# An instruction scheduler inside a kernel: forward and backward passes, durations nearer to the trace, and a new place for the late weight loads

## The chip, the cores and the metric

One core of a Trainium2 chip runs the whole program in one launch. The metric is the device time of one execution in microseconds. A first group of three runs of the kernel before gave a median of 398.55 us (397.55 to 398.92). Executions are compared within one state. All runs told here had a mean granted TensorE clock of 0.994 to 1.0 and are in the fast state; a program that was run only once has no state, and that is said where it comes. A mean of 0.996 is not the same as one of 1.0, though: in the kernel before such runs are slower by 1.7 us, as the part on calls 2 and 3 shows.

Five engines work in parallel: TensorE (PE in the profile) multiplies matrices into PSUM; ScalarE (ACT) and VectorE (DVE) read PSUM and work on SBUF; GpSimd (POOL) works on SBUF; SyncE (SP) only issues DMA transfers here. Each has its own list of instructions and waits on semaphores for the others. The order of those five lists is what this change is about.

## The reference

Two attention layers and two feed-forward (GLU) layers alternate, each with a layer norm before it and a residual addition after it. The sequence is 2048 rows of 512 columns, all in bfloat16.

```python
def _A_ref(x, wqkv, w_phi, wo):            # H = 32 heads of 16
    q, k, v = ...                          # x @ wqkv, split in heads
    pq = einsum("bhsd,hdf->bhsf", q, w_phi); pk = einsum(... k, w_phi)
    phi_q = concat([softmax(pq), softmax(-pq)]); phi_k = the same of pk
    kv  = einsum("bhsf,bhsd->bhfd", phi_k, v)      # needs every key row
    num = einsum("bhqf,bhfd->bhqd", phi_q, kv)
    den = einsum("bhqf,bhf->bhq", phi_q, sum of phi_k over s) + 1e-6
    return (num / den) ... @ wo
def _B_ref(x, W_gate, W_up, W_down):       # 512 -> 1376 -> 512
    gate = x @ W_gate; gate = gate * (gate > 0)
    return (gate * (x @ W_up)) @ W_down
# ...
x = x + _A_ref(_layernorm(x), ...);  x = x + _B_ref(_layernorm(x), ...)
x = x + _A_ref(_layernorm(x), ...);  x = x + _B_ref(_layernorm(x), ...)
```

One fact of it shapes everything below: `kv` sums over all 2048 rows, so no row can get its `num` before the last key tile has been through its softmax. The first attention layer therefore has a key stage, then a narrow place, and only then the long streams of GLU matmuls.

## The kernel before

The program is written as a list of operations. Each names its engine, what it reads and writes, and a duration in nanoseconds that the author gives it. A scheduler then simulates the five engines with these durations and so decides the order of each engine's list. Nothing else of the simulation reaches the chip; only the order does. The scheduler of before goes through the program once, with one ranking:

```python
class Program:
    ORDER_WEIGHT = 20.0
    DMA_BW = 300.0
    # ...
    def schedule(self):
        # ...
        rank = [0.0] * n                  # the longest way from here to the end
        for o in reversed(ops):
            rank[o.idx] = o.dur + max([rank[q] + lat(o, ops[q]) for q in succ[o.idx]], default=0.0)
        prio = [self.ORDER_WEIGHT * o.idx - rank[o.idx] - o.boost for o in ops]
        # ... one forward pass: of what can start soonest, take the lowest prio
```

The parts whose durations the change touches, and the loads whose place it touches:

```python
    # normalising the keys: the whole tile on POOL, for the last two tiles half on DVE
    parts = [("pool", 0, 2)] if t < NT - 2 else [("pool", 0, 1), ("dve", 1, 2)]
    # ... expk = expk * rZk
       (1930 if s1 - s0 == 2 else 980) if eng == "pool" else 620, f"{tag} phik {t} {s0}")
# ...
    # layer norm's "apply" on DVE: ytile = x * rstd - mean * rstd
       [r("x", t), r("mv", t), r("rstd", t)], [r("yt", yb)], 407, f"{tag} apply {t}")
# ...
        def kv(t, n):                     # emit(): key tiles t .. t+n-1
            # ... projections
            for tt in range(t, t + n):
                self.kv_acc(tt, "A0")
                for _ in range(2):        # two late weight loads per key tile
                    if pieces:
                        pieces.pop(0)(self.r("phik", tt, 0))
        # ...
        kv(10, 2)
        self.q_proj(0, qr0, "A0")         # queries of the first 512 rows
        kv(12, 2)
        kv(14, 1)
        kv(15, 1)
        self.kv_fin("A0")                 # kvbd: kv out of PSUM, masked
        for li in (0, 2):
            # ...
            N([0, 1, 2, 3])               # num, divide, wo, residual, layer norm
            for st in range(1, NSLAB):
                self.q_proj(st, qring, A, [self.r("expk", 15, 1)], w=2)
            # ... then GLU steps mixed with the rest of the num steps
```

The late weights (`pieces`) are the twenty-two loads of wo, Wg, Wu and Wd that are not needed at the start. Each is held back until a given key tile has been normalised.

The softmax here doesn't subtract the row's maximum and nothing guards it: scores larger than these inputs give would overflow.

## Time and profile before

| | before |
|---|---|
| median of 3 runs | 398.55 us |
| the profiled run, and its span in the trace | 397.03 us, 395.1 us |
| TensorE busy | 380.4 us (96%), 2320 matmuls |
| VectorE, ScalarE, GpSimd busy | 274.2, 217.5, 111.2 us |
| DMA | 23 MB, 58 GB/s over the span |

Most of the reading of this profile is in the prediction below. Two views are added here, because the result turns on them. In a timeline the columns are start in us, length in us, engine, line and operation, the tiles, how many in a row, and in brackets the engine's idle time before it and what ended it. The first is the timeline of ACT just after the keys of the first layer. L590 is the exponential of the queries, and L607 is the copy of `num` out of PSUM, three copies to a tile.

```profile
55.06 1.02 ACT L590 ACTIVATE expq<-ps 128x1024 bf16<-128x1024 f32 x1 [3.37 <-PE ps L587]
55.98 1.32 ACT L607 ACTIVATE numbf<-ps 128x432 bf16<-128x432 f32 x3
57.20 1.02 ACT L590 ACTIVATE expq<-ps 128x1024 bf16<-128x1024 f32 x1
58.10 0.96 ACT L607 ACTIVATE numbf<-ps 128x432 bf16<-128x432 f32 x2
59.26 0.41 ACT L607 ACTIVATE numbf<-ps 128x288 bf16<-128x288 f32 x1 [0.19 <-PE ps L603]
```

ACT stands idle for 3.37 us, then does one exponential, the three copies of tile 0, another exponential, and the three copies of tile 1. The second is the timeline of TensorE near the end, the down projections of the last GLU:

```profile
383.67 2.98 PE L678 MATMUL ps<-Wd,hT 128*128 128x512 bf16 x13
386.99 4.93 PE L678 MATMUL ps<-Wd,hT 128*128 128x512 bf16 x22 [0.34 <-DVE x_sb L680]
```

TensorE waits there for a residual addition to clear a PSUM bank.

### The profile page before, as it was taken

To read this page: it belongs to the slowest core of one execution; us is meant where nothing else is said; L and a number is where in the kernel's file an instruction comes from. 1 tells how busy PE (TensorE), PEld (TensorE's weight loads), DVE (VectorE), ACT (ScalarE), POOL (GpSimd) and SP (SyncE) were. 2 spreads that over 40 slices of the span, in tenths; PEclk is the share of its full clock that TensorE was granted. 3 is DMA by queue.
4 is the path that set the end of the run, shared out by engine and by line. 5 is a ranking of instruction groups with operands and counts; after the bars stand their busy time and mean duration, and the time that the engine had idled before them with its cause. 6 is when DMAs were issued, how large, how long until landed. Compare 5 with 4: busy or idle time off the path is not lost.

```text
span 395.1 us, 6306 instructions
## 1 busy us (share of the span) xinstructions
PE 380.4 (96%) x2320; PEld 206.0 (52%) x2320; DVE 274.2 (69%) x634; ACT 217.5 (55%) x421; POOL 111.2 (28%) x160
## 2 busy tenths in 40 slices
PE   5999987999999999999999999899999999999996
PEld 3445543676744544444444467467774454444442
DVE  4999868778767898887747876977776677222222
ACT  5989759753735513532454483996474562452440
POOL 5389931112000213373334552120301101000000
PEclk9999999999999999999999999999999999999999
DMA  6845841322211222301000110231322132100001
GB/s 208 207 87 126 258 135 27 68 53 55 42 40 27 42 41 57 73 18 28 13 13 2 27 28 2 44 73 32 75 56 60 40 42 66 42 13 26 2 27 53
DMA packets 61518, 23.00 MB, mean 58 GB/s; under 512 B 53456, under 2 KB 60464, under 8 KB 61488
## 3 DMA queue, kind: packets, MB, share of 16 engines
q1 hardware_dynamic: 60912, 22.08, 24.1%
q10 hardware_dynamic: 576, 0.52, 0.5%
q8 instruction: 18, 0.29, 0.3%
q14 instruction: 12, 0.10, 0.1%
HBM read 7.91 MB, written 2.10 MB: 25 GB/s over the span
## 4 chain that ended last, share of the span: by engine, by line
PE 86%; DMA 4%; DVE 3%; ACT 3%; issue 2%; POOL 1%; ACTq 0%; SPq 0%; DVEq 0%
PE ps L654 39%; PE ps L678 19%; PE ps L633 7%; PE ps L514 7%; PE ps L587 5%; PE ps L603 3%; PE ps L545 3%; PE ps L560 2%; DMA x_sb<-in_A_x_dram 2%; ACT expk L548 1%; DMA yT<-ytile 1%; DMA hT<-in_A_wqkv_dram 1%; ACT expq L590 1%; DVE expk L531 1%; ACT numbf L607 1%
## 5 line engine op out<-in xcount | busy, mean ns | idle before, releaser
L654 PE MATMUL ps<-yT,Wg 128*128 128x512 bf16 (+3 forms) x440 | 127.6, 336 | 0.0
L654 PE MATMUL ps<-yT,Wu 128*128 128x512 bf16 (+3 forms) x440 | 124.0, 336 | 0.0
L678 PE MATMUL ps<-Wd,hT 128*128 128x512 bf16 (+1 forms) x352 | 107.9, 379 | 0.3 <-DVE x_sb L680 0.3
L656 ACT ACTIVATE gate_sb<-ps 128x512 bf16<-128x512 f32 (+3 forms) x110 | 56.4, 514 | 93.8 <-PE ps L654 85.5
L478 POOL TENSOR_SCALAR rv<-mv 128x1 f32<-128x1 f32 (+1 forms) x55 | 14.1, 258 | 192.2 <-DVE mv L475 192.2
L531 POOL TENSOR_TENSOR expk<-expk,rZk 128x1024 bf16<-128x1024 bf16 (+1 forms) x32 | 59.6, 1879 | 27.0 <-DVE rZk L528 21.1
L654 PEld LDWEIGHTS ps<-yT,Wu 128*128 128x128 bf16 (+1 forms) x440 | 43.9, 100 | 33.2 <-ACT expk L661 0.9
L654 PEld LDWEIGHTS ps<-yT,Wg 128*128 128x128 bf16 (+1 forms) x440 | 43.5, 100 | 33.5 <-ACT gate_sb L656 0.6
L607 ACT ACTIVATE numbf<-ps 128x432 bf16<-128x432 f32 (+1 forms) x96 | 44.9, 496 | 19.9 <-PE ps L603 19.1
L678 PEld LDWEIGHTS ps<-Wd,hT 128*128 128x128 bf16 (+1 forms) x352 | 34.2, 98 | 37.1 <-DVE x_sb L680 1.0
L663 DVE TENSOR_TENSOR hT<-gate_sb,expk 128x512 bf16<-128x512 bf16 (+3 forms) x73 | 25.8, 354 | 32.5 <-ACT expk L661 32.4
L474 DVE BATCH_NORM_STATS2 stats<-x_sb 128x6 f32<-128x512 bf16 x64 | 42.6, 680 | 5.5 <-DMA x_sb<-in_A_x_dram 5.2
L526 DVE TENSOR_REDUCE Zk<-expk 128x64 f32<-128x1024 bf16 x32 | 38.1, 1205 | 6.6 <-ACT expk L517 5.2
L633 PE MATMUL ps<-wo_p,oT 128*128 128x512 bf16 x128 | 38.8, 379 | 0.5 <-DMA oT<-osb 0.5
L603 PE MATMUL ps<-kvbd,expq 128*128 128x144 bf16 x256 | 35.8, 226 | 2.0 <-ACT numbf L607 1.5
L590 ACT ACTIVATE expq<-ps 128x1024 bf16<-128x1024 f32 (+1 forms) x40 | 32.7, 863 | 8.5 <-PE ps L587 8.4
L587 PE MATMUL ps<-yT,Wqp 128*128 128x512 bf16 x128 | 35.8, 379 | 1.7 <-ACT expq L590 1.7
L661 ACT ACTIVATE expk<-ps 128x512 bf16<-128x512 f32 (+3 forms) x73 | 36.3, 498 | 1.6 <-PE ps L654 1.0
L680 DVE TENSOR_TENSOR x_sb<-x_sb,ps 128x512 bf16<-128x512 bf16 x32 | 21.6, 683 | 21.5 <-PE ps L678 21.2
L479 POOL TENSOR_TENSOR rstd<-rv,mhalf 128x1 f32<-128x1 f32 (+1 forms) x55 | 34.1, 621 | 4.1
L666 DVE TENSOR_TENSOR hT<-gate_sb,ps 128x512 bf16<-128x512 bf16 (+2 forms) x37 | 22.6, 611 | 16.3 <-PE ps L654 12.2
L517 ACT ACTIVATE expk<-ps 128x512 bf16<-128x512 f32 x44 | 23.7, 602 | 18.2 <-PE ps L514 18.0
(57 smaller groups left out, 400.1 us busy)
## 6 DMA issues: line engine op xcount, KB each, us to landing
out_dram<-x_sb SPq DMA_DIRECT2D x16, 128.0 KB, 1.7
x_sb<-in_A_x_dram SPq DMA_DIRECT2D x3, 512.0 KB, 6.6
Wg<-in_B_W_gate_dram SPq DMA_DIRECT2D x4, 344.0 KB, 3.6
Wu<-in_B_W_up_dram SPq DMA_DIRECT2D x4, 344.0 KB, 6.0
Wd<-in_B_W_down_dram SPq DMA_DIRECT2D x5, 256.0 KB, 7.0
yT<-ytile SPq DMA_TRANSPOSE x60, 2.4
hT<-in_A_wqkv_dram ACTq DMA_DIRECT2D x4, 128.0 KB, 3.0
x_sb<-in_A_x_dram SPq DMA_DIRECT2D x4, 128.0 KB, 3.7
```

What stands on the lines that cost most here:

```text
L474: op("dve", (lambda t: lambda e: e.bn_stats(k.stats6[:, t, :], k.x_sb[:, t, :]))(t), [r("x", t)], [r("st", t)], 685, f"{tag} stats {t}")
L526: op("dve", lambda e: e.tensor_reduce(k.Zk[:, zb, :], k.expk[:, t, :, :].rearrange("p s (h f) -> p (s h) f", f=16), AX.X, ALU.add), [r("ex ...
L531: op(eng, (lambda s0, s1: lambda e: e.tensor_tensor(k.expk[:, t, s0:s1, :].rearrange("p s (h f) -> p (s h) f", f=16), k.expk[:, t, s0:s1, ...
L587: op("pe", (lambda c, ic, bank: lambda e: e.matmul(k.pb[bank][:], k.Wqp[:, ic, c * 128:(c + 1) * 128], k.yT[:, ic, st * 512:(st + 1) * 512 ...
L590: op("act", (lambda c0, s, b0: lambda e: e.activation(k.expq[:, st, c0:c0 + w, s, :], k.ps[:, b0:b0 + w, :], ACT.Exp, scale=(1.0 - 2.0 * s ...
L603: op("pe", (lambda s, c, j, g0, bank: lambda e: e.matmul(k.pb[bank][:, j * GW:(j + 1) * GW], k.expq[:, st, c, s, tt * 128:(tt + 1) * 128], ...
L607: op("act", (lambda g0, n, bank: lambda e: e.activation(k.numbf[:, b, g0:g0 + n, :], k.pb[bank][:, 0:n * GW].rearrange("p (g m) -> p g m", ...
L633: op("pe", (lambda c, bank: lambda e: e.matmul(k.pb[bank][:], k.oT[:, ob, c, :], k.wo_p[:, c, :], start=(c == 0), stop=(c == NC - 1)))(c, ...
L654: op("pe", (lambda bank, W, ic, fc, Mf: lambda e: e.matmul(k.pb[bank][0:Mf, 0:n], W[:, ic, fc * 128:fc * 128 + Mf], k.yT[:, ic, c0:c0 + n] ...
L656: op("act", (lambda Mf, gb, gs: lambda e: e.activation(k.gate_sb[0:Mf, gs, 0:n], k.pb[gb][0:Mf, 0:n], ACT.Relu))(Mf, gb, gs), [self.RP[gb] ...
L661: op("act", (lambda Mf, ub, tu: lambda e: e.activation(k.expk[0:Mf, tu, 0, 0:n], k.pb[ub][0:Mf, 0:n], ACT.Copy))(Mf, ub, tu), [self.RP[ub] ...
L678: op("pe", (lambda fc, Kf, u, c0: lambda e: e.matmul(k.pb[bank][:], k.hT[0:Kf, u, c0:c0 + 128], k.Wd[0:Kf, fc, :], start=(fc == 0), stop=( ...
```

## The change

The change has three parts, and none adds, removes or resizes an operation.

1. **A search in place of one pass.** Four weights of the ranking start it. For each, a forward pass makes a schedule; a backward pass then schedules the same program from its end and gives each operation a time at which it would come if everything were as late as it can be; these times are the ranking of the next forward pass. There are twelve passes for each weight, 48 in all, and the schedule with the shortest simulated time is kept.
2. **Durations set nearer to those of the trace.** A few operations and loads get other durations in the model, among them the key multiply on DVE (1050 instead of 620 ns; in the trace of before it takes from 0.69 to 2.03 us) and the DMA bandwidth (240 instead of 300 bytes per ns).
3. **Late weights over more key tiles.** Tiles 4 to 11 release one late load each instead of two.

```diff
-    ORDER_WEIGHT = 20.0
-    DMA_BW = 300.0
+    ORDER_WEIGHTS = (5.0, 10.0, 20.0, 30.0)
+    PASSES = 12
+    DMA_BW = 240.0
@@ schedule
-        prio = [self.ORDER_WEIGHT * o.idx - rank[o.idx] - o.boost for o in ops]
+        best = None
+        for weight in self.ORDER_WEIGHTS:
+            prio = [weight * o.idx - rank[o.idx] - o.boost for o in ops]
+            for _ in range(self.PASSES):
+                start, finish, order = self._forward(prio)
+                span = max(finish)
+                if best is None or span < best[0]:
+                    best = (span, start, finish, order)
+                prio = [t - o.boost for t, o in zip(self._backward(start, finish), ops)]
 (... _forward is the old pass, made a function; _backward is new)
@@ durations
-        ... (t1 - t0) * 131072, f"dma x{t0}")
+        ... 131072 * (t1 - t0) if t1 > t0 + 1 else 96000, f"dma x{t0}")
 (wk loads 131072 -> 96000 bytes; WqT's issue 5000 -> 7000; two ACT copies 530 -> 600)
-               (1930 if s1 - s0 == 2 else 980) if eng == "pool" else 620, f"{tag} phik {t} {s0}")
+               (1930 if s1 - s0 == 2 else 980) if eng == "pool" else 1050, f"{tag} phik {t} {s0}")
-               [self.RP[bank], r("mask8")], [r("kvbd", bank)], 700, f"{tag} kvbd {bank}")
+               [self.RP[bank], r("mask8")], [r("kvbd", bank)], 550 if n == 3 else 430, f"{tag} kvbd {bank}")
@@ late weights
-                for _ in range(2):
+                for _ in range(1 if 4 <= tt < 12 else 2):
```

## The prediction

> **What bounds the kernel now.** I read the page's first two parts first, to see which engine carries the span.
>
> ```profile
> PE 380.4 (96%) x2320; PEld 206.0 (52%) x2320; DVE 274.2 (69%) x634; ACT 217.5 (55%) x421; POOL 111.2 (28%) x160
> ...
> PE   5999987999999999999999999899999999999996
> ...
> PEclk9999999999999999999999999999999999999999
> ```
>
> TensorE is marked busy for 96% of the span at full granted clock; the idle tenths stand at the start, in slices 6 and 7 (about 50 to 69 us), in one slice past the middle and at the end. But a modelled matmul end makes busy time too kind, so I counted the work by pitch. In the chain of waits nineteen 512-column matmuls of L654 take 4.10 us, 216 ns each, while the groups list one as 379 ns. From the groups kept apart by shape there are 1392 matmuls of 512 columns, 352 of 256, 256 of 144, 256 of 129 and 64 of 128. With the smallest usual start-to-start distance of each in this trace (216, 109, 63, 57 and 56 ns) they need 300.7 + 38.4 + 16.1 + 14.6 + 3.6 = 373.4 us. The span is 395.1. It opens with 3.2 us before the first matmul (waiting for the first weights) and closes with 3.2 us after the last (residual add and store). So 395.1 - 373.4 - 6.4 = 15.3 us are lost between the first and last matmul. No reordering can win more than that. Next, where it is lost, by stages:
>
> ```profile
> core 0: us, PE busy (x) PEld busy (x) DVE busy (x) ACT busy (x) POOL busy (x), PEclk, DMA share, GB/s
> 3.20:17.00 13.80, 11.94 (x81) 6.95 (x82) 11.27 (x29) 11.05 (x20) 6.10 (x13) 1.00 0.93 255
> 17.00:30.00 13.00, 12.72 (x78) 6.06 (x76) 13.00 (x27) 11.17 (x17) 10.05 (x10) 1.00 0.44 92
> 30.00:52.00 22.00, 20.67 (x168) 12.11 (x165) 20.64 (x25) 17.96 (x27) 21.91 (x15) 1.00 0.77 214
> 52.00:70.00 18.00, 15.14 (x104) 7.84 (x105) 13.24 (x41) 14.08 (x24) 3.08 (x5) 1.00 0.17 42
> ...
> 80.00:225.00 145.00, 145.00 (x792) 75.14 (x790) 110.77 (x243) 63.97 (x133) 44.47 (x64) 1.00 0.18 35
> 225.00:250.00 25.00, 23.33 (x222) 15.06 (x221) 17.11 (x37) 16.19 (x31) 8.42 (x8) 1.00 0.11 22
> 250.00:386.00 136.00, 136.00 (x786) 73.93 (x787) 77.63 (x213) 75.29 (x160) 13.74 (x32) 1.00 0.19 42
> ```
>
> The two long stages, 281 us together, are full: start-to-start distances there show under 0.3 us lost. Everything else is lost in five places. By start-to-start distance less the pitch: 4.7 us in the opening to 17 us, 3.2 us in the key stage of the first attention layer (17 to 52), 4.1 us from 52 to 70 (first normalised tiles until the GLU's matmuls begin), 2.4 us at the second layer's same place (225 to 250), 0.5 us near 386. In the key stage DVE and POOL are the full engines, not PE. What ends the waits:
>
> ```profile
> 52.34 0.62 PE L560 MATMUL ps<-vsb,expk 128*128 128x129 bf16 x8 [1.19 <-DVE expk L531]
> ```
> ```profile
> PE ps L587 <- ACT expq L590: 1.7, 2, 1.5
> PE ps L560 <- DVE expk L531: 1.2, 1, 1.2
> PE ps L603 <- ACT numbf L607: 0.4, 1, 0.4
> ```
>
> The first is the last key normalisation; the three others are PE's waits in 52 to 70: after the keys, PE waits for ACT to clear PSUM banks. In 225 to 250 it is 1.1 us for ACT (numbf) and 0.4 us for the transposed output tile. The POOL and DVE timelines of the key stage show why the keys end at 53 us:
>
> ```profile
> 19.86 7.69 POOL L531 TENSOR_TENSOR expk<-expk,rZk 128x1024 bf16<-128x1024 bf16 x4
> 29.29 0.23 POOL L478 TENSOR_SCALAR rv<-mv 128x4 f32<-128x4 f32 x1 [1.73 <-DVE mv L475]
> ...
> 35.04 18.06 POOL L531 TENSOR_TENSOR expk<-expk,rZk 128x1024 bf16<-128x1024 bf16 x10
> ```
> ```profile
> 31.05 1.65 DVE L491 TENSOR_SCALAR ytile<-x_sb,mv,rstd 128x512 bf16<-128x512 bf16 x1
> ...
> 34.62 0.33 DVE L491 TENSOR_SCALAR ytile<-x_sb,mv,rstd 128x512 bf16<-128x512 bf16 x1
> ```
>
> POOL runs without a break from 35.0 to 53.1 us, after one hole of 1.73 us in which it waited for DVE's statistics of the last four x tiles. And the same DVE operation takes 0.33 us beside a small POOL one but 1.65 us beside a POOL multiply, ending just as that multiply ends.
>
> **What the Trainium skill says.** "TensorE: Matmul & The Clock Gate", section "Back-to-back issue gap", gives an isolated 512-column gap of about 216 ns warm; this trace has 216. (The same section's lower sustained figure, 131 ns, isn't seen here.) "SBUF — State Buffer", section "Who interferes with whom", says VectorE's tensor_scalar in a two-port mode, and its two-input tensor_tensor against GpSimd's reads, contend with GpSimd for a port pair held for the whole instruction, the loser fully blocked. The trace agrees: 1.65 against 0.33 us above, and the last two DVE multiplies (L531) take 2.03 and 1.54 us at 48.7 us beside POOL, but 0.69 us in the second layer. "Perfetto Trace Analysis", section "Identifying the Most-Contended Engine", advises interleaving stages whose contended engine differs; that is what is left to win here.
>
> **The change, part by part.** No operation is added, removed or resized: 2320 matmuls stay, so the 373.4 us stay, and so does the granted clock. Only the order on each engine and the time of the late weight loads move. The scheduler tries 48 forward passes and keeps the one its own model likes best; I take no time from that model.
>
> 1. *Opening.* The built order differs little: the same transposes, copies and composed weights, with tile 0's exponentials now before the last two yT copies (one ACT copy is 0.6 us). The first matmul still waits for the load at 3.2 us; the composed key weights still alternate DVE and ACT copies. I allow 0.3 us.
>
> 2. *Key stage.* All DVE statistics are now before the third Zk, and POOL's third group of rstd stands after its first multiply instead of its fourth: the 1.73 us hole shrinks or moves to where POOL is not yet late. Against that, four applies on DVE (tiles 8, 10, 12, 14) now lie among POOL multiplies; before, two of these four did (1.19 and 1.65 us) and two took 0.31 and 0.33. Two more blocked ones cost about 2 x 1.0 = 2.0 us of DVE time, and DVE had only 1.36 us of idle here (at 41.1 us, waiting for ACT's exponentials). So DVE may replace POOL as the bound. Working both: POOL -1.7, DVE +2.0 - 1.4 = +0.6; I take the mean, about -0.5, and another -0.3 for late weights: from tiles 4 to 11 one load per tile instead of two, so that fewer sit ahead of the yT transposes (one issue took 3.46 us at 37.8 against 1.19 usual). Sum -0.8 us.
>
> 3. *52 to 70.* The new ACT order puts numbf of tiles 0 and 1 (six copies, 2.6 us) ahead of the first paired expq (1.02 us); before, one expq stood ahead of each. The chain numbf, six DVE steps, transpose, wo, residual, layer norm, transpose to the first GLU matmul (73.2 us) begins 1.0 us sooner for tile 0 and 2.0 for tile 1. But 12 expq and 18 numbf still stand before the first gate: 12 x 0.97 + 12 x 0.49 + 6 x 0.36 (from their starts) is 19.7 us, and ACT ran from 55.06 to 75.0 with about 1.3 us idle. ACT itself can thus give only 1.3. I take -1.0 us.
>
> 4. *Second layer's same place.* The order of numbf was already so. PE now runs 53 key accumulations and then waits for kvbd (0.55 + 0.18 us plus the way there, about 0.9 us), where before four q matmuls (0.86 us) filled it; these come later as filler instead, and kvbd of the first bank is now finished before the second starts (about 0.5 us sooner). Net -0.4 us.
>
> 5. *End.* Thirty-eight down matmuls in a row instead of forty, in the same banks; the 0.5 us wait for the residual at 386 may go: -0.2. The final add and store (3.2 us) stay. *New small waits* in the full stages, whose order has changed everywhere: +0.4.
>
> Sum: -0.3 - 0.8 - 1.0 - 0.4 - 0.2 + 0.4 = -2.3 us, so 398.55 - 2.3 = about 396.2; I say 396.0, since a list chosen as the best of 48 with truer durations is more likely to find a little more than I see than a little less.
>
> **Rivals.** (a) *DVE becomes the bound of the key stage*: the model gives an apply 407 ns whatever POOL does. For it: 1.65 us blocked, DVE already 20.6 of 22 us busy. Against: its 1.36 us idle. If all blocked applies count and nothing else is won, the kernel is +1 to +2 us, 399.5 to 400.5. (b) *The waits all go*: the truer durations let PE be fed everywhere outside the opening; of 15.3 us lost, 4.7 in the opening stay, and ACT's need in part 3 leaves about 2: a gain of up to 8 us, 390.5. Against: two of the five places are bounded by the work of DVE, POOL and ACT, which stays. (c) *A late weight makes the GLU or its down projection wait*, as the loads now come after later tiles. Against: Wg and Wu follow tiles 4 to 11, done on POOL by about 47 us, 26 us before the first GLU matmul at 73; Wd follows tiles 12 to 14, done by 53, needed at 88, with a time to landing of 7 us. Hidden either way: 0.
>
> **Range and chances.** The losses that a reorder could touch are about 10 us and at best some 8; a gain of 2% needs 8.0 us (390.6), so it takes rival (b) whole. A loss of 2% needs 8 new microseconds in stages that have queues of ready matmuls. Three runs of before spread over 1.4 us. Eighty per cent: 392.3 to 399.5. Chances: faster by over 2% 0.05, within 0.93, slower 0.02.
>
> **What would show it.** Right: PE's work unchanged at 2320; in the windows, the key stage and 52 to 70 fuller by 1 to 2 us together; POOL's 1.73 us wait gone; DVE's applies of 1.2 to 1.7 us four in number before 52 us; the first paired expq after six numbf and the first Wg matmul at 71 to 72.5 us; the two full stages still without waits. Wrong: a first Wg matmul past 73 (the DVE rival), matmuls that start at 108 or 216 ns pitch with holes after 80 us (new waits), or the opening shortened by over 1 us, which I hold fixed.

## The result, and the profile after

| | before | after |
|---|---|---|
| median (lowest to highest, runs) | 398.69 us (397.55 to 398.92, 4) | 396.08 us (395.31 to 396.79, 4) |
| ratio of the fast runs, 95% interval | | 0.994 (0.9913 to 0.9967) |
| the profiled run, and its span | 397.03, 395.1 us | 395.86, 394.1 us |

All ratios in this document are the mean time of one kernel's fast runs over the mean of the other's fast runs of the same rounds, so they are not quite the ratios of the medians beside them. The change is faster by 2.6 us in the medians, 0.6%. That is "same" at the 2% level, and close to the 396.0 us that were predicted. Whether the working behind that number was right is another question, and the two traces answer it.

The page of the kernel after, with busy time by engine and the busy tenths of TensorE in forty slices:

```profile
PE 381.1 (97%) x2320; PEld 207.1 (53%) x2320; DVE 274.3 (70%) x634; ACT 215.8 (55%) x421; POOL 110.1 (28%) x160
...
PE   5998997999999999999999999899999999999996
```

The counts of instructions are the same, as they must be. Slice 4 is emptier than it was, slice 6 has filled up to nine tenths, and the dip at slice 26 and the end look the same. By stages, in the columns that the prediction's table has:

```profile
30.00:52.00 22.00, 20.57 (x158) 11.58 (x159) 18.93 (x25) 15.99 (x23) 19.79 (x11) 1.00 0.75 195
52.00:70.00 18.00, 15.46 (x113) 8.40 (x112) 14.17 (x43) 14.40 (x25) 3.75 (x6) 1.00 0.31 80
...
80.00:225.00 145.00, 145.00 (x793) 75.56 (x791) 108.58 (x241) 62.28 (x131) 43.45 (x64) 1.00 0.18 34
225.00:250.00 25.00, 24.04 (x228) 15.47 (x226) 18.08 (x40) 17.09 (x33) 8.44 (x8) 1.00 0.11 22
250.00:386.00 136.00, 135.85 (x787) 73.86 (x784) 79.15 (x212) 73.11 (x157) 14.15 (x32) 1.00 0.19 42
```

In the key stage DVE, ACT and POOL are all less busy than before (18.93, 15.99 and 19.79 us of 22; before 20.64, 17.96 and 21.91), and yet TensorE is no busier (20.57 against 20.67). Nobody was at a limit there; they waited for one another.

Fixed windows have a weakness here: the two kernels do different work in the same window, because the order moved. So I put **anchors** at events that both kernels have, took the time from anchor to anchor, and subtracted the matmuls that the program has between them at the pitches of the prediction. What remains is time in which TensorE was not fed, or ran below its full pitch. Three traces of each kernel were taken in the end (two of each come from the experiments below). Lost time in us, the three traces and their mean:

| from, to | before | mean | after | mean | change |
|---|---|---|---|---|---|
| start, first matmul | 3.21, 3.24, 3.12 | 3.19 | 3.12, 3.15, 3.13 | 3.13 | -0.06 |
| first matmul, first matmul with kvbd | 8.23, 8.99, 7.72 | 8.31 | 9.53, 8.76, 9.35 | 9.21 | +0.90 |
| from there to the first gate matmul (Wg) | 3.90, 3.87, 3.89 | 3.89 | 3.05, 3.04, 3.06 | 3.05 | -0.84 |
| first gate matmul, second layer's key sums | 0.13, 1.25, 0.12 | 0.50 | 0.04, 0.04, 0.05 | 0.04 | -0.46 |
| from there to the second layer's first gate matmul | 2.40, 2.40, 2.40 | 2.40 | 1.89, 1.89, 1.89 | 1.89 | -0.51 |
| from there to the last matmul | 0.67, 0.66, 0.66 | 0.66 | 0.12, 0.12, 0.12 | 0.12 | -0.54 |
| start of the last matmul, end | 3.55, 3.56, 3.55 | 3.55 | 3.39, 3.39, 3.39 | 3.39 | -0.16 |

The changes add up to -1.67 us, which is the difference of the mean spans (395.5 and 393.85). Two things stand out. The second and third rows together lost 12.20 us before and 12.26 after: **the whole first attention layer gave nothing**. And a good part of what was gained is in rows where the prediction expected little or a loss.

The second row is not all waiting. In the opening TensorE runs at half its later pitch, as the same four transposes show at two times in the kernel before:

```profile
7.97 0.63 PE L499 MATMUL ps<-ident,ytile 128*128 128x128 bf16 x4
9.58 0.39 PE L499 MATMUL ps<-ident,ytile 128*128 128x128 bf16 x4
```

From start to start a matmul of 128 columns takes 107 ns in the first and 56 in the second. The half pitch ends about where the trace's first record of the full clock begins: at 8.8, 11.8 and 9.1 us in the three traces of before, and at 12.8, 9.5 and 13.1 us in those of after. (Before that record a view prints a clock of 1.00 only because it has none.) The losses of the row follow this: 8.23 and 7.72 us with an early full clock and 8.99 with a late one before; 8.76 with an early one and 9.53 and 9.35 with a late one after. Like against like, the change costs about 0.45 to 0.8 us in this row and not 0.90. And about half of it is lost before the keys are well under way: in the mean 4.92 us before and 5.91 after are lost up to 17 us, and 5.79 and 6.26 up to 30 us.

Look first at POOL in the key stage (timeline, kernel after):

```profile
21.97 0.23 POOL L520 TENSOR_SCALAR rv<-mv 128x4 f32<-128x4 f32 x1 [0.45 <-DVE mv L517]
...
41.68 3.81 POOL L573 TENSOR_TENSOR expk<-expk,rZk 128x1024 bf16<-128x1024 bf16 x2 [0.62 <-DVE rZk L570]
47.08 6.74 POOL L573 TENSOR_TENSOR expk<-expk,rZk 128x1024 bf16<-128x1024 bf16 x4 [1.59 <-ACT expk L559]
```

The hole of 1.73 us is now one of 0.45, as predicted. But two new holes of 0.62 and 1.59 us have come, and the last key multiply ends at 47.08 + 6.74 = 53.82 us, where before it ended at 53.10. (The other two traces of after have such holes of 0.29 and 1.31, and of 0.78 and 1.09 us.) DVE in the same stage, kernel after:

```profile
28.41 1.33 DVE L533 TENSOR_SCALAR ytile<-x_sb,mv,rstd 128x512 bf16<-128x512 bf16 x1
...
38.73 2.35 DVE L568 TENSOR_REDUCE Zk<-expk 128x64 f32<-128x1024 bf16 x2 [0.88 <-ACT expk L590]
44.13 2.34 DVE L568 TENSOR_REDUCE Zk<-expk 128x64 f32<-128x1024 bf16 x2 [2.19 <-ACT expk L590]
...
54.26 1.02 DVE L613 TENSOR_TENSOR kvbd<-ps,mask 128x384 bf16<-128x384 f32 x2 [1.36 <-PE ps L602]
```

The blocked apply is there (1.33 us; the three others took 0.48, 0.78 and 0.78). But DVE also stands idle for 0.88 and 2.19 us, waiting for ACT's exponentials, which wait for TensorE's key projections. In this window TensorE itself waited 1.2 us for transposed tiles (yT). So the keys are late by a loop through all engines. Then ACT after the keys, to be held against the same place before:

```profile
55.83 1.37 ACT L649 ACTIVATE numbf<-ps 128x432 bf16<-128x432 f32 x3 [1.79 <-PE ps L645]
57.41 1.37 ACT L649 ACTIVATE numbf<-ps 128x432 bf16<-128x432 f32 x3 [0.21 <-PE ps L645]
58.67 1.02 ACT L632 ACTIVATE expq<-ps 128x1024 bf16<-128x1024 f32 x1
```

The order is as predicted: six copies of `num` come before the first paired exponential. But tile 0's copies end at 57.20 us, and before they ended at 57.30. The exponential that stood in front of them before had run while ACT would have waited anyway, since the third copy waits for matmuls that TensorE started at 56.56 us before and at 56.46 after; now ACT waits 1.79 us there. Tile 1's copies end at 58.78 against 59.67 us. And the first gate matmul, before and after:

```profile
73.24 0.27 PE L654 MATMUL ps<-yT,Wg 128*128 128x256 bf16 x1
```
```profile
74.85 0.27 PE L696 MATMUL ps<-yT,Wg 128*128 128x256 bf16 x1
```

It starts later (74.85, 74.10 and 74.69 us in the three traces of after; 73.24, 74.00 and 72.63 in those of before). That alone is no loss: subtracting lost time from elapsed time gives 57.90 us of matmul work ahead of it before (73.24 - 3.21 - 12.13) and 59.15 after (74.85 - 3.12 - 12.58), so 1.25 us more work had been done by then. In the same way 0.87 us less work, four 512-column matmuls of q, lies before the first kvbd matmul. These matmuls now fill the next stretch, and that is why the second row of the table got worse and the third better.

The gains that are real are further on. TensorE's waits from 225 to 260 us in the kernel after, as engine, what waited, for what, then total, times and longest:

```profile
PE ps L675 <- DMA oT<-osb: 0.8, 1, 0.8
```

Before there were 1.1 us for ACT's copies and 0.4 us for the transposed output tile; the first is gone. And the end of the kernel after:

```profile
383.74 7.39 PE L720 MATMUL ps<-Wd,hT 128*128 128x512 bf16 x33
```

Thirty-three down projections run without a break where before there was a wait after thirteen.

### The profile page after: what moved, and what is told of

The parts are those of the page before. It is cut to its first block, busy times and chain, and to the rows that moved or that the text cites. A ratio compares the mean times of both kernels' runs of the same rounds, so it can differ in the third digit from the quotient of the medians.

```text
span 394.1 us, 6313 instructions
## 1 busy us (share of the span) xinstructions
PE 381.1 (97%) x2320; PEld 207.1 (53%) x2320; DVE 274.3 (70%) x634; ACT 215.8 (55%) x421; POOL 110.1 (28%) x160
## 4 chain that ended last, share of the span: by engine, by line
PE 83%; DVE 7%; issue 3%; DMA 3%; ACT 2%; POOL 2%; SPq 0%; DVEq 0%; POOLq 0%
PE ps L696 39%; PE ps L720 19%; PE ps L556 7%; PE ps L675 7%; PE ps L629 5%; PE ps L645 3%; PE ps L602 2%; DVE stats L516 2%; POOL expk L573 2%; DVE rZk L570 1%; DMA yT<-ytile 1%; DVE Zk L568 1%; DMA x_sb<-in_A_x_dram 1%; ACT numbf L649 1%; DMA oT<-osb 1%
## 5 line engine op out<-in xcount | busy, mean ns | idle before, releaser
L696 PE MATMUL ps<-yT,Wu 128*128 128x512 bf16 (+3 forms) x440 | 128.2, 336 | 0.0
L520 POOL TENSOR_SCALAR rv<-mv 128x1 f32<-128x1 f32 (+1 forms) x55 | 13.0, 238 | 190.1 <-DVE mv L517 187.7
L649 ACT ACTIVATE numbf<-ps 128x432 bf16<-128x432 f32 (+1 forms) x96 | 44.1, 500 | 18.1 <-PE ps L645 16.9
L675 PE MATMUL ps<-wo_p,oT 128*128 128x512 bf16 x128 | 39.9, 379 | 1.6 <-DMA oT<-osb 1.6
L629 PE MATMUL ps<-yT,Wqp 128*128 128x512 bf16 x128 | 34.7, 379 | 0.9 <-ACT expq L632 0.7
```

The costliest lines, as they stand in the source:

```text
L629: op("pe", (lambda c, ic, bank: lambda e: e.matmul(k.pb[bank][:], k.Wqp[:, ic, c * 128:(c + 1) * 128], k.yT[:, ic, st * 512:(st + 1) * 512 ...
L649: op("act", (lambda g0, n, bank: lambda e: e.activation(k.numbf[:, b, g0:g0 + n, :], k.pb[bank][:, 0:n * GW].rearrange("p (g m) -> p g m", ...
L675: op("pe", (lambda c, bank: lambda e: e.matmul(k.pb[bank][:], k.oT[:, ob, c, :], k.wo_p[:, c, :], start=(c == 0), stop=(c == NC - 1)))(c, ...
L696: op("pe", (lambda bank, W, ic, fc, Mf: lambda e: e.matmul(k.pb[bank][0:Mf, 0:n], W[:, ic, fc * 128:fc * 128 + Mf], k.yT[:, ic, c0:c0 + n] ...
```

## The experiments

Twelve entries were run in three calls, four of them the kernel before or after once more. Within a call all run on one chip and share the runs of the kernel before, whose median was 398.85 us in the first call (48 runs, 396.85 to 401.4), 399.29 in the second (11 runs, 398.43 to 400.75) and 398.74 in the third (15 runs, 396.62 to 401.07). Every kernel gave a correct result. The expectations name theories by letters, each spelled out there: S is the search and D the durations (with the late loads) as what pays; T is that late loads hold back the transposes of the key stage; L is the port that DVE and POOL share.

### Call 1: which part pays

**`after_again`** is the kernel after, word for word.

> The changed kernel again, word for word, for a second trace and a tighter ratio. Theory N (the opening's extra 1.5 us in the first trace of after is noise of loads and of the slow first matmuls): the loss up to 17 us comes out nearer to the 4.7 us of before, and the run at a ratio of 0.991 to 0.994. Rival O (the new order of the opening costs it): the loss up to 17 us is again 5.8 to 6.4 us. Either way the last key multiply on POOL ends at 53.5 to 54.1 us, not earlier than the 53.1 of before.

Measured: 395.64 us (395.15 to 396.45, 6 runs), ratio 0.9928 (0.9902 to 0.9954). The result repeats. Up to 17 us this trace loses 5.07 us, nearer to the 4.74 of before than to the 6.23 of the first trace of after; so most of that extra was a draw (theory N), and the draw goes with the full clock, which set in at 9.5 us here and at 12.8 there. The last key multiply ends at 52.89 us, sooner than either theory had it.

**`passes_only`** has the new search, with the durations, the bandwidth and the late loads of before:

```diff
 (against after)
-    DMA_BW = 240.0
+    DMA_BW = 300.0
-    ... else 1050, f"{tag} phik {t} {s0}")
+    ... else 620, f"{tag} phik {t} {s0}")
 (and the other durations of the change, each back to its old value)
-                for _ in range(1 if 4 <= tt < 12 else 2):
+                for _ in range(2):
```

> The new scheduler (four rankings, twelve forward and backward passes each) with the old durations, the old bandwidth and the old late weights. Theory S (the search makes the gain): ratio 0.991 to 0.996, as good as the whole change within 1 us. Rival D (the truer durations make it): ratio 0.998 to 1.003.

Measured: 397.07 us (396.11 to 398.01, 21 runs), ratio 0.9959 (0.9944 to 0.9973).

**`durations_and_late_only`** is the opposite: the old single pass with the new durations, bandwidth and late loads.

```diff
 (against before)
-    DMA_BW = 300.0
+    DMA_BW = 240.0
 (and every duration of the change, and the late loads)
```

> The old single forward pass with the new durations, bandwidth and late weights. Theory S: within 0.8 us of before, ratio 0.998 to 1.002. Rival D: ratio 0.993 to 0.997.

Measured: 396.46 us (395.75 to 397.69, 12 runs), ratio 0.9943 (0.9924 to 0.9962).

**`without_late`** is the whole change except that each key tile releases two loads again.

```diff
-                for _ in range(1 if 4 <= tt < 12 else 2):
+                for _ in range(2):
```

> The whole change but for the late weights, which stay at two per key tile. If spreading them was worth the 0.3 us that I gave it, this is 0.3 us slower than the whole change (395.9 to 396.9 in its median, ratio about 0.995). If the loads that stand ahead of the yT transposes on SP are what held the end of the keys at 53 to 54 us, two per tile (all issued by tile 10) puts more of them ahead, PE's waits for yT between 17 and 52 us grow from 1.8 us to over 2.5, and the kernel loses 1 us or more against the whole change.

Measured: 396.57 us (395.31 to 399.27, 22 runs), ratio 0.9947 (0.9928 to 0.9967).

What follows. In medians against 398.85, the search alone gives 1.8 us, the durations with the late loads alone give 2.4, and all together 3.2. But these medians mix two kinds of execution: those with a mean granted clock of 0.999 to 1.0, and slower ones with 0.994 to 0.996 (more on them under calls 2 and 3). Of the slower kind were 25 of the 48 runs of before, none of the 21 of `passes_only`, 2 of 12 of `durations_and_late_only`, 1 of 6 of `after_again` and 10 of 22 of `without_late`. At 0.999 to 1.0 alone the medians are 397.81 us before, 397.07 with the search, 396.38 with the durations and the late loads, and 395.64 with all: gains of 0.7, 1.4 and 2.2 us. There the two halves do add up, and the durations are the larger. Theory S falls (it had the search alone within 1 us of the whole, and 1.4 us are missing), while D, which falls by a little on all runs (0.9959 where it had 0.998 to 1.003), is about met at the full clock: 0.998 and 0.996 in the medians.

Leaving out the late loads costs 0.9 us in the medians of all runs, and 0.2 us (395.88 against 395.64) at 0.999 to 1.0; so nearly all of it is the slower kind of run, and 10 of 22 against 1 of 6 is too little to say that the late loads bring it on. In its one trace TensorE's waits for yT from 17 to 52 us did grow, to 3.3 us from 1.2 to 2.1 in the three traces of after, as the expectation had it; the loss of 1 us at the full clock did not follow in the medians.

The traces, one of each, show where the halves act. The search wins the tail (3.39 us, where the old pass has 3.55 with either set of durations) and some of the second layer's narrow place (1.86 us against 2.40), but with the old durations it gives more than that back in the first GLU and near the end (1.02 us lost before the last matmul, against 0.66). With the durations alone no row stands out: 11.92 us up to the first gate matmul, within the 11.61 to 12.86 of before's three traces, then 0.50, 2.19 and 0.58. These are TensorE's waits from 70 to 100 us in `passes_only`:

```profile
PE ps L696 <- DMA oT<-osb: 0.8, 1, 0.8
PE ps L675 <- DMA oT<-osb: 0.6, 1, 0.6
```

The first is booked to a gate matmul, but a matmul of the output projection comes right behind it. By the anchors 1.74 us are lost there, where after loses 0.04. The search puts the output projection of a tile close behind its transpose, as close as its model allows, and in this trace two transposes landed too late for that.

### Calls 2 and 3: the kernels before and after once more

**`before_again`** and **`before_third`** are the kernel before, run once for a trace, so with no state; **`after_beside`** is the kernel after.

> The kernel before, word for word, for a second trace of it. By the work on TensorE up to a given matmul, the first trace of before lost 8.2 us between its first matmul and the first matmul with kvbd (55.1 us), two traces of after lost 9.5 and 8.8. Theory A (the first trace of before is a quick draw of the opening, as its run was 1.6 us under the median): this trace loses 9 to 10.5 us there, and the same as the first one, within 0.2 us, in every later stretch (3.9, 0.1, 0.1, 2.4, 0.7). Rival B (the new order really costs 0.5 to 1.3 us before the first kvbd matmul): it loses 8.0 to 8.5 us again.

> The kernel before, for a third trace. One of its two traces lost 1.1 us at 95 us, where TensorE waited for a transposed output tile (oT), and the other nothing. If that wait comes and goes with the landing of one transpose and is usual in slow draws: a run at 398.4 us or more shows a wait of 0.5 us or more there, a run at 397.5 or less does not.

> The changed kernel once more, on the same chip as the two above, as their measure: ratio 0.991 to 0.994. Lost time in its trace: 0.0 to 0.1 us between the first gate matmul and the second layer's keys, 3.0 us between the first kvbd matmul and the first gate matmul, 1.8 us at the second layer's place, as in both traces so far; only the stretch before the first kvbd matmul may differ (8.8 and 9.5 so far).

Measured: 398.91 us and 396.41 us (one run each), and for `after_beside` 395.74 us (394.51 to 398.22, 7 runs), ratio 0.9921 (0.9887 to 0.9956). The slower of the two single runs shows a wait that neither of the other traces of before has. Its timeline of TensorE at 95 us:

```profile
95.49 0.27 PE L654 MATMUL ps<-yT,Wg 128*128 128x256 bf16 x1
96.72 0.82 PE L633 MATMUL ps<-wo_p,oT 128*128 128x512 bf16 x3 [0.95 <-DMA oT<-osb]
```

In the first trace of before the transpose of this tile is issued at 92.1 us and its first matmul starts at 94.85, which is 2.75 us later, against a usual 2.4 us from issue to landing: 0.35 us of slack, so that nothing is seen. In this trace the transpose is issued at 92.8 us and takes 3.8 us to land. The order of before leaves a thin margin there, and one trace in three pays 1.1 us for it. All three traces of after lose 0.04 or 0.05 us in that row. Of the expectations, theory A and rival B of `before_again` both miss: it loses 8.99 us before the first kvbd matmul, between the two ranges, with a full clock that set in 3 us later than in the first trace. `before_third` (a fast run, no wait at 95 us) and `after_beside` come out as expected.

This bears on the size of the result. Medians differ by 2.6 to 3.2 us, the mean spans of the traces by 1.65, and the fastest run of each kernel over all calls (396.41 and 394.51 us) by 1.9. The three traced runs of before took 397.03, 398.91 and 396.41 us, so two of them were well under its medians, while those of after (395.86, 395.15, 395.73) are within 0.5 us of its own.

**What the slower half of before's runs loses** can be read from the granted clock that is on record for each run. In call 1, 25 of the 48 runs of before had a mean clock of 0.996 and a median of 399.54 us; the 23 others had 0.999 or 1.0 and a median of 397.81. One trace of this study, that of `q1_and_lock` in call 3 (mean clock 0.994), shows what such a mean can hide. A row of its windows, in the columns of the prediction's table:

```profile
63.20:66.60 3.40, 3.40 (x13) 1.47 (x13) 2.13 (x5) 2.54 (x6) 0.00 (x0) 0.50 0.19 39
```

For 3.4 us the clock was at a half. A matmul of 512 columns took 427 ns from start to start there instead of 216, and 1.7 us were lost. In the 3.2 us just before, TensorE was busy for only 1.69 us; that this brought it on is not shown. One such stretch in 395 us makes a mean of 0.996 and costs what the slower runs of before lose, so they most likely hold one. Where, is not known: the three traces of before had means of 0.999 to 1.0. (In some traces the clock is also at a half for the last 0.4 to 1.1 us, behind the last matmul, where no matmul is left to slow down.)

In the three calls 37 of 74 runs of before were of this kind, and 2 of the 17 runs of after that this document has; those two, 395.18 and 396.29 us, were no slower than the rest, so such a mean does not always cost time. As an estimate from these medians, about 1 of the 3.2 us of call 1 is that such stretches are rarer after the change. At 0.999 to 1.0 the medians differ by 2.2 us in call 1 (397.81 and 395.64, 23 and 5 runs) and by 2.9 in call 3 (398.62 and 395.74, 8 and 7). The clock is not all of the spread: one run of `after_beside` at 1.0 took 398.22 us.

### Call 2: what holds the first layer

**`late_after_keys`** releases no late load before tile 8 and three per tile from there. If late loads ahead of the yT transposes were what holds the keys, they should be done sooner.

```diff
-                for _ in range(1 if 4 <= tt < 12 else 2):
+                for _ in range(3 if tt >= 8 else 0):
```

> The changed kernel with no late weights before key tile 8 and three per tile from there, so that nearly all yT transposes are issued ahead of the loads. Theory T (in the changed kernel the key stage is held by yT that comes late, behind loads on SP that wait for POOL's multiplies): PE's waits for yT between 29 and 50 us (1.8 and 1.7 us in the two traces) fall under 0.5 us, the keys end 0.5 to 1 us sooner, the kernel gains 0.5 to 1.2 us (ratio 0.988 to 0.991). Rival P (POOL and DVE hold it, whatever comes when): the keys end where they did, 53 to 54 us, and the time is that of the changed kernel within 0.5 us or worse (the scheduler's own model has it 1.1 us longer).

Measured: 394.97 us (394.14 to 397.52, 6 runs), ratio 0.9901 (0.9874 to 0.9927). TensorE's waits for yT from 29 to 52 us fell to 0.7 us (1.2, 1.4 and 1.3 in the traces of after), but the lost time up to the first gate matmul is 12.12 us, against a mean of 12.26, and the last key multiply ends at 53.25 us (53.82, 52.89 and 53.65 in the traces of after). Against the mean the mechanism of theory T is not seen. Against the two traces of after whose full clock set in as late as here (13.1 us) the keys end 0.6 and 0.4 us sooner and 0.5 and 0.3 us less are lost, which is the direction of T, in one trace. So T is not settled. The time is 0.7 to 1.1 us below the medians of after, with overlapping intervals; where that would come from is not settled.

**`model_with_lock`** teaches the model what the traces show of DVE and POOL: of a DVE apply or a key multiply on either engine, the one that starts later lasts until the other is done and then its own time. The key multiply of DVE gets its free duration of 690 ns back.

```diff
+            dur = o.dur
+            if o.lock:      # DVE apply, key multiplies on DVE and POOL
+                dur += max(0.0, held["pool" if o.eng == "dve" else "dve"] - st)
+                held[o.eng] = st + dur
-            free[o.eng] = st + o.dur
+            free[o.eng] = st + dur
-    ... else 1050, f"{tag} phik {t} {s0}")
+    ... else 690, f"{tag} phik {t} {s0}").lock = True
```

> The changed kernel, its scheduler told that a DVE apply or key multiply cannot run beside a POOL key multiply (the later one waits for the earlier). Nothing else is different. Theory L (the blocked applies, missing in the model, are what keeps the keys from ending at the modelled 52.4 us): the schedule that knows them ends the keys earlier than the 52.9 and 53.8 us measured, and the kernel gains 0.5 to 1.5 us (0.987 to 0.992). Rival (1.7 us of blocked DVE time lie beside 3.1 us in which DVE waits anyway, so they cost nothing): no gain, ratio 0.992 to 0.998.

Measured: 394.70 us (394.54 to 395.31, 5 runs), ratio 0.9888 (0.987 to 0.9907). POOL's timeline at the end of the key stage:

```profile
35.71 13.29 POOL L579 TENSOR_TENSOR expk<-expk,rZk 128x1024 bf16<-128x1024 bf16 x7
50.13 2.52 POOL L579 TENSOR_TENSOR expk<-expk,rZk 128x512 bf16<-128x512 bf16 x2 [1.13 <-DVE rZk L576]
```

The keys end at 50.13 + 2.52 = 52.65 us, and 11.68 us are lost up to the first gate matmul, 0.6 less than after's mean and 0.1 less than after's best trace. That best trace had an early full clock (9.5 us, here 13.0); against the two with a late one 0.9 and 0.7 us less are lost. That is mild support for theory L: one trace, and a time 0.9 to 1.4 us below the medians of after, with an interval that overlaps those of two of its three measurements.

**`q1_in_key_stage`** does not touch the scheduler. It moves the query projection of the second 512 rows, with its eight exponentials on ACT, from behind the keys into the key stage. By the prediction's part 3 ACT has too much to do after the keys, and the windows show it less busy before: 15.99 us of 22.

```diff
         self.q_proj(0, qr0, "A0")
+        self.q_proj(1, qr0, "A0")
         kv(12, 2)
 ...
-            for st in range(1, NSLAB):
+            for st in range(1 if li else 2, NSLAB):
                 self.q_proj(st, qring, A, [self.r("expk", 15, 1)], w=2)
```

> The changed kernel with the first layer's q projection of slab 1 put into the key stage (one bank, eight expq of 0.6 us), where ACT has about a fifth of its time idle, and taken from the stage of the first normalised tiles. Theory Q (that stage is held by ACT's 12 paired expq and 18 numbf): it loses less than 2.0 us between the first kvbd matmul and the first gate matmul instead of 3.05, that gate matmul comes 2 to 4 us sooner, and the kernel gains 0.5 to 1.5 us. Rival C (the chain of one tile through numbf, DVE, transposes and wo holds it, and the q matmuls were its filler): the loss there rises to 4 us or more, and the time is the same or up to 1.5 us worse.

Measured: 393.80 us (393.13 to 394.62, 6 runs), ratio 0.9867 (0.9847 to 0.9887). Its windows and its first gate matmul:

```profile
30.00:52.00 22.00, 21.70 (x172) 12.64 (x171) 20.31 (x26) 17.64 (x27) 21.89 (x13) 1.00 0.89 205
52.00:70.00 18.00, 16.48 (x125) 9.37 (x123) 14.22 (x43) 15.46 (x30) 2.24 (x5) 1.00 0.30 75
```
```profile
71.43 0.27 PE L696 MATMUL ps<-yT,Wg 128*128 128x256 bf16 x1
```

The first gate matmul starts at 71.43 us. Lost time up to it is 9.16 us (7.08 up to the first kvbd matmul, 2.08 from there), 3.1 less than after's mean; 0.8 us of that are given back right behind it, 0.83 us lost where after loses 0.04: about 0.3 us at a wait for an exponential at 72.6 us and 0.4 us at one for a transposed output tile at 73.8. Two mechanisms lie in this run. The sixteen moved matmuls fill TensorE's holes among the keys (2.1 us less lost there than in the mean, 1.7 less than in the trace of after whose full clock set in as early). And the narrow place becomes shorter by 2.3 us (54.28 to 71.43 is 17.15 us, after 55.43 to 74.85 is 19.42): 1.3 us of that is less matmul work and 1.0 us less lost time, although sixteen matmuls that could fill its holes, 3.5 us, are gone. If a lack of filler had held TensorE there, its lost time would have grown; so this speaks for ACT's queue, which the edit shortened too. The expectation is met but for two sizes: 2.08 us lost where it had under 2.0, and a gain of about 2 us over after where it had 0.5 to 1.5. This is the best kernel of the study, faster than before and after.

### Call 3: do the gains add

**`q1_and_lock`** and **`q1_and_late`** join the moved queries with each of the two other edits; their diffs are those above.

> The slab 1 q projection in the key stage and the scheduler that knows the blocked DVE and POOL multiplies, together. Theory I (the two act in different places: the lock before the first kvbd matmul, the q projection mostly after it): about 1 us under the q projection alone, ratio 0.982 to 0.986. Rival (both use up the same slack of the key stage): no better than the q projection alone, 0.985 to 0.990.

> The slab 1 q projection in the key stage, and no late weights before key tile 8. If the loads ahead of the yT transposes cost what the run with late weights after the keys seemed to show (0.7 to 1.1 us, with intervals that overlap), 0.983 to 0.986; if that was chance, 0.986 to 0.989.

Measured: 396.41 us (395.36 to 398.34, 9 runs), ratio 0.9938 (0.9917 to 0.996) for the first, and 395.25 us (394.89 to 395.55, 4 runs), ratio 0.9899 (0.9872 to 0.9927) for the second. Neither reaches the moved queries alone. With the lock 6.01 us are lost from the first kvbd to the first gate matmul (2.08 without it), of which 1.7 us are the stretch at half clock shown above, and another 1.02 us before the last matmul (0.12 without). The medians agree without such runs: 396.38 us at 0.999 to 1.0 (7 of its 9 runs). The best schedule found under one input differs from that under another over the whole program, not only where the edit is: here the losses moved at both ends. So the gains of such edits need not add up.

## Why the prediction was right or wrong

The total was right: 396.0 us predicted, 396.08 measured, and a range of 392.3 to 399.5 that held every run of after. The working was right in less than that. The table goes by the traces, all at a mean clock of 0.999 or 1.0; the prediction also held the granted clock fixed, and that failed for half of the runs of before: by the estimate above about 1 us of the 3.2 between the medians of call 1 is that stretches at half clock became rarer.

| step | predicted | in the traces (means) |
|---|---|---|
| 1 to 3, opening, key stage and 52 to 70 | -2.1 | +0.06 |
| 4, the second layer's same place | -0.4 | -0.51 |
| 5, the end | -0.2 | -0.70 (-0.54 before the last matmul, -0.16 behind it) |
| new small waits in the full stages | +0.4 | -0.46 (with before's one slow trace; -0.08 without it) |
| start to the first matmul | held fixed | -0.06 |
| sum | -2.3 | -1.67 |

**Step 1 failed.** It allowed a gain of 0.3 us in the opening. Up to 17 us 5.91 us were lost after and 4.92 before, in the means; with an early full clock 5.07 against 4.74 and 4.72, with a late one 6.23 and 6.42 against 5.30. By 30 us the difference of the means is down to 0.5 us. Which part of the new order costs this was not tested.

**Step 2 failed**, in the way that "POOL -1.7, DVE +2.0 - 1.4" was put together. The hole of 1.73 us did go, and the four blocked applies came, with 0.48, 1.33, 0.78 and 0.78 us. But together they are 3.37 us, where the four of before took 1.65 + 1.19 + 0.31 + 0.33 = 3.48: more of them are blocked, each for a shorter time, so the "+2.0" measured -0.1. With POOL's hole gone and no cost on DVE the stage should by this step have become shorter, and it did not. What the step had wrong is its picture of a stage with two full engines, in which what they gain moves the end. The trace of after shows a loop instead: keys through TensorE, ACT, DVE and POOL, x tiles through DVE, a transpose and TensorE. When POOL's one hole closed, two others opened, of 2.2 us together in that trace. DVE waited for ACT for 3.1 us, so rival (a), DVE as the bound, did not happen either. That the late yT transposes are the cause was tried and is not settled; that the shared port is a part of it has one run in its favour.

**Step 3 failed** in its sentence that the chain "begins 1.0 us sooner for tile 0 and 2.0 for tile 1". It began 0.1 and 0.9 us sooner. The exponential that before had in front of tile 0's copies cost nothing, because ACT was waiting for the kvbd matmuls then; taking it away left an idle time of 1.79 us. The other half of the step, that ACT's queue bounds this stage and can give little, was right, and `q1_in_key_stage` supports it. (Its sum is off: 19.7 us of work and 1.3 of idle time do not fit into the 19.94 us from 55.06 to 75.0; the trace has ACT busy for 18.51.) The anchors' -0.84 us in this stretch looks like the predicted -1.0 but is not it: four matmuls of q moved from the stretch before it to fill this one. My own sign of failure was a first gate matmul past 73 us, and it came at 74.1 to 74.85. I had tied that sign to the DVE rival; the criterion was poor, because the order also put 1.25 us more work ahead of that matmul.

**Step 4 was right**: -0.51 for -0.4, and the 1.1 us wait for ACT's copies is gone. A wait of 0.8 us for the transposed tile is what is left.

**Step 5 had the right mechanism and was mis-sized.** The wait for the residual near 386 us is gone, and with it 0.54 us, for which 0.2 was allowed as a chance that it "may go". The tail behind it fell by 0.16 us.

**The new small waits had the wrong sign.** I read one trace of before, in which the two full stages were full, and so took it that a new order could only do harm there. Another trace of the same kernel shows a wait of 0.95 us at 95 us for a transpose that landed late. The new order has no such thin margin in its three traces.

So the prediction reached the right total by luck in its terms: about 2 us expected in the first layer did not come, and some 1.5 us more than expected came elsewhere (0.1 in step 4, 0.5 in step 5, 0.9 in the full stages). Rival (b), that all waits go, was far off: after still loses 14.3 us between the first and the last matmul, against 15.8. Rival (c), a late weight that holds up the GLU, did not happen: no wait for a late weight is in any of after's three traces.

What stays open: what makes the loop of the key stage as long as it is; where the 0.7 to 1.1 us of `late_after_keys` come from; where in the slower half of before's runs the clock drops, and why it does so more rarely after the change.

## What to carry to other kernels

Count what an engine loses between events that both kernels have, not in fixed windows, before you call a fuller window a gain: a reorder moves work over the edge of every window. Before taking an instruction out from in front of a critical one, look whether the engine would have been idle there anyway. And when a scheduler's order is already close to its own model's best, as here (of the orders of this one program, each timed by its own model while it was built, `passes_only` came out shortest, and on the chip it was the slowest but for before), giving the program itself another order to start from, as the moved queries do, was worth about 2 us, about as much again as the whole change. Last, look at the granted clock of every run before you divide a gain among its parts: here a mean of 0.996 instead of 1.0 made two halves that add up look as if they did not.

## What the Trainium skill lacked or had wrong

- "TensorE: Matmul & The Clock Gate", section "Back-to-back issue gap", calls 216 ns for 512 columns the isolated gap and gives 131 ns (and about 81 ns for 128 columns) as the sustained one in a stream of loads and matmuls. Here, in just such a stream of 2320 loads and 2320 matmuls, 512 columns take 216 ns and 128 columns 56 ns once the clock is full (107 ns for 128 columns in the opening), so the page's isolated formula is the one that holds.
- "SBUF — State Buffer", section "Who interferes with whom", has the rule that the later one of DVE and POOL is blocked, and the traces agree, but it does not say how to put this in a cost model. Here the same DVE apply takes from 0.33 us beside a small POOL operation to 1.65 us behind a POOL multiply; and a half key multiply on POOL takes 1.50 us when DVE's started 0.11 us earlier (236.88 and 236.99 us, DVE's taking 0.69), where the kernel's own model has 0.98.
- "DMA: Bandwidth & Descriptors", section "Latency and other measured facts", gives DMA transposes a bandwidth (261 GB/s) but no spread of their time to landing. Here a 128 KB transpose inside SBUF lands after 2.4 us in the median, and one wanted at 95 us took 3.8 us in one trace and 2.4 in another of the same kernel; among the yT transposes the slowest took 5.4 to 5.9 us in the six traces. A schedule with 0.35 us of slack behind such a transfer is not safe.
- No page says how far executions of one single-core kernel differ. Here 48 runs of the kernel before on one chip spread from 396.85 to 401.4 us: from 396.85 to 399.19 at a mean granted clock of 0.999 to 1.0, and from 398.68 to 401.4 at 0.996. Thirteen of after on two chips spread from 394.51 to 398.22. One trace of a kernel does not show which of its waits is paid every time.
